# First set's weights converted one at a time, prepared weights fetched three products ahead, PSUM tiles evicted by one engine each

## The chip, the cores and the metric

The kernel runs on one core of a Trainium2 chip. The metric is device time in microseconds (us) of one execution. Engines are named as in the profile: PE (TensorE matmuls), PEld (TensorE weight loads), DVE (VectorE), ACT (ScalarE), POOL (GpSimd), and SP (SyncE), which here only issues DMAs; POOL issues accumulating DMAs as well. Each engine, and the DMA queue of SP and of POOL, works in its own program order.

## The reference

```python
def _attn_ref(q, k, v, omega):            # q, k, v: (4, 8, 576, 64); omega: (128, 64)
    ...                                   # phi(x) = exp(x omega^T - |x|^2/2 - max) / sqrt(m)
    kv = np.einsum('bhsm,bhsd->bhmd', k_p, v)
    z = np.sum(k_p, axis=2)
    num = np.einsum('bhsm,bhmd->bhsd', q_p, kv)
    den = np.einsum('bhsm,bhm->bhs', q_p, z)[..., None] + 1e-06
    return num / den

def _moe_ref(x, w_gate, w_val, w_out):    # x: (2304, 512); weights (512, 1536) and (1536, 512)
    g = x @ w_gate
    silu = g * (1.0 / (1.0 + np.exp(-g)))
    val = x @ w_val
    return (silu * val @ w_out).astype(np.float32)

def _moe2_ref(x, w_gate, w_val, w_out):   # the same with sigmoid alone as the gate
    ...

x = attention output as (2304, 512);  return _moe2_ref(_moe_ref(x))
```

The weights of both layers arrive as 64-bit floats and are converted to 32 bits on the chip.

## The kernel before

Attention runs first, in an order written out by hand. The 2304 tokens are then cut into three sets of 768, and each set passes through layer 0 and layer 1. A matmul of 32-bit values is done as three matmuls of a high and a low part: a copy on ACT makes the high part, a subtraction on DVE the low part (class `Split`, lines 238 and 242).

**The first set of layer 0** (the loop over `c` at line 783, 12 steps, one for each 128 columns of `d_ff`) multiplies directly. In a step PE computes two gate products (`first`, 12 matmuls of 384 columns each; ACT reads them for the SiLU into `s`, line 806), two value products (DVE multiplies `s` by them, line 812), and then `second` for the step before, which adds that step's part of the output into the six `acc` tiles. The four products of a step share two PSUM buffers (`ps_g`), so a product can start only when the product two before it has been read. ACT then makes `hh` of `s`, and DVE makes `hl`.

In the same loop the layer's weights are converted (class `Weight`): 26 units of 128x512, each loaded as 512 KB (`load`, line 136, into three `wraw` buffers), then `magnitude` on ACT (line 151, into one of four `wtmp` buffers), then `bits`, `sign`, `power` and `term` on DVE (lines 157, 164, 171, 177), and `total`, an accumulating DMA issued by POOL (line 183), which must land before the `wtmp` buffer is free again. Two or three units belong to a step, and they stand together at its end, each operation for all of them before the next operation. DVE also makes sums of weights (`sums`, line 214), and SP stores these and the weights to DRAM (`wf`, `ws`).

**The other five sets** (two of layer 0, three of layer 1) use Strassen products. For each of six `p` there are seven products `k` (line 950, 12 matmuls each, 42 in a set), then 12 steps of the output product (line 735 in layer 0, lines 260 to 262 in layer 1). PSUM holds two `X` tiles, one `Y` and one `Z`, of two banks each. Weights come back from DRAM: `fetch(o)` (line 714, SP, 256 KB, three `wp` buffers) and `prepare(o)`, which makes `vh` on ACT and `vl` on DVE. `prepare(o + 3)` is called at product `o` and fetches two further. Between the products the generator `make_second` converts layer 1's weights, one operation at a time. At a set's end `result` copies the six accumulators out, ACT and DVE in turn (lines 757 and 755); in layer 1 lines 1008 and 1010 do so.

Of the kernel before, what the change touches and what calls it, by code (L numbers as in the profile page):

```python
# [32 lines left out]
def tile_performer_attention__then__two_glu_layers(  # L33
# [230 lines left out]
    def first(ab, w, x, o):  # L264

        cols = slice(ab * TS, (ab + 1) * TS)
        for kk in range(KC):
            three(o, [u[:, kk, :] for u in w], [u[:, cols] for u in x[kk]], kk == 0, kk == KC - 1)
        return o
# [397 lines left out]
    }  # L667
    xc, xt, fetched, ready = {}, {}, {}, {}
    sequence = [
# [39 lines left out]
    def fetch(o):  # L709
        if o < len(sequence) and o not in fetched:  # L710
            l, p, k = sequence[o]
            t = fetched[o] = late.tile([P, 2 * H2], F32, tag="wp", bufs=3, name="wp")
            src = w_second[l][k] if p is None else w_first[l][p][:, k].rearrange("p n f -> p (n f)")
            nc.sync.dma_start(out=t, in_=src)

    def prepare(o):
        if o < len(sequence) and o not in ready:
            fetch(o)
            tags = slots[2 * (o % RING):2 * (o % RING) + 2]
            hi, lo = [wres.tile([P, 2 * H2], F32R, tag=x, name="v" + n) for x, n in zip(tags, "hl")]  # L720
            ready[o] = Split(fetched.pop(o), hi, lo).both()
            fetch(o + 1)
            fetch(o + 2)

# [22 lines left out]
    def result(acc, n, j):  # L747

        cols = set_of(n)
        src, dst = acc[j], xx[:, j % KC, cols.start:cols.start + MAIN]  # L750
        if j >= KC:
            src = src.rearrange("p (j t) -> p j t", j=2)
            dst = xx[:, 2 * (j - KC):2 * (j - KC) + 2, cols.start + MAIN:cols.stop]
        if j % 2:
            nc.vector.tensor_copy(dst, src)
        else:
            nc.scalar.activation(dst, src, AF.Copy)

    make = [[] for _ in range(FC)]
    for i, u in enumerate(units[0]):
        make[i * (FC - 3) // (len(units[0]) - 1)].append(u)
    done = {u.key for _, u in early}
# [11 lines left out]
    with tc.manual_schedule():  # L776
        for u in make[0]:
            u.load()
        prev = None
        acc = [ps_a.tile([P, MAIN], F32, tag=f"acc{j}", name="acc") for j in range(6)]  # L780
        late = pool("late", 1, side="right")
        for c in range(FC):
            for o, i in stores[c]:
                store(o, i)
            us = make[c]

            def part(us, *fs):
                for f in fs:
                    for u in us:
                        f(u)  # L790


# [9 lines left out]
            hl = hsb.tile([P, 2, TS], F32R, tag="hl", name="hl")  # L802
            place_of = lambda: ps_g.tile([P, TS], F32, tag="g", name="pg")
            for i in range(2):
                g = begun.pop(0) if begun else first(i, w[0], x, place_of())
                nc.scalar.activation(s[:, i], g, AF.Silu)  # L806
            values = [first(i, w[1], x, place_of()) for i in range(2)]
            for u in ahead:
                u.both()
            w2.both()  # L810
            for i in range(2):
                nc.vector.tensor_tensor(s[:, i], s[:, i], values[i], ALU.mult)
            nc.scalar.activation(hh, s, AF.Copy)
            t = wsum.tile([P, 4, H2], F32, tag="s", name="wsums")
            *_, then = sums(*pair, t)
            for o, i in then:
                store(o, i)
            nc.vector.tensor_tensor(hl, s, hh.bitcast(F32), ALU.subtract)
            x_parts(1, c - 2)
            part(us, Weight.magnitude, Weight.bits, Weight.sign, Weight.power, Weight.term)  # L820
            for u in us:
                u.total(True)
                store_later(c + 2, u)
                done.add(u.key)
            for u in make[c + 1] if c + 1 < FC else []:
                u.load()
            w2 = w2.parts
            w = w_next or [u.parts for u in ahead]
            if c >= FC - AHEAD:
                prepare(c + AHEAD - FC)  # L830
            if prev is not None:
# [6 lines left out]
        for j in LAST:  # L838
            result(acc, 0, j)
        for c in (FC - 2, FC - 1):  # L840
            x_parts(1, c)

# [3 lines left out]
        makers.close()  # L846
        wraw, wtmp, made = pool("wraw2", 2), pool("wtmp2", 3), pool("made", 1)
        ps_yz, ps_x = pool("ps_yz", 1, space=PSUM), pool("ps_x", 2, space=PSUM)
        tmp, hall = pool("tmp", 1), pool("hall", 1)
# [44 lines left out]
        def make_second():  # L894

            us, todo = units[1], []
            for u in us[:1]:
                u.load()
            yield
            for i, u in enumerate(us):  # L900
# [32 lines left out]
        for at, (layer, n) in enumerate(STRASSEN):  # L933
            h, hs = {}, {}
            ahead = STRASSEN[at + 1][1] if at + 1 < len(STRASSEN) else None
            for p in range(FC // 2):
# [5 lines left out]
                for k in range(7):  # L942
# [35 lines left out]
                    if p == FC // 2 - 1 and k in (3, 5):  # L978
                        c = (k - 3) // 2
                        hs[c] = h_split(c)  # L980
            acc = [bank(ps_yz, "Y"), bank(ps_yz, "Z"), bank(ps_x, "X")]
            acc = [t[:, i, :] for t in acc for i in range(2)]
# [19 lines left out]
            for b in range(6):  # L1002
# [3 lines left out]
                t = tmp.tile([P, DM], F32, tag=("u2", "p5", "s0", "s2")[b % 4], name="o")  # L1006
                if b % 2:
                    nc.scalar.activation(t, acc[b], AF.Copy)
                else:
                    nc.vector.tensor_copy(t, acc[b])  # L1010
# [46 lines left out]
```

## Time and profile before

| | us |
|---|---|
| median of three runs | 1054.29 (1053.64 to 1056.53) |
| the profiled execution, its own time | 1055.49 |
| its span from first to last instruction | 1053.7 |
| PE busy in the span | 1019.9 (97%) |
| DVE busy | 752.0 (71%) |
| ACT busy | 595.7 (57%) |

What the profiled execution takes beside its span is 1.79 us. PE's share of busy time is so high that only its gaps can be removed; where they lie is read from windows of the span, and what ends them from the waits and the timeline. The attention part ends at about 176 us of the span, the first set at about 344 us, and the last matmul starts at 1046.4 us.

### The profile page before, as it was taken

How to read it: one execution, taken by the hardware profiler on the slowest of the kernel's cores; microseconds unless marked ns; L12 is line 12 of the kernel's file. 1: busy time of each engine (PE TensorE's matmuls, PEld its weight loads, DVE VectorE, ACT ScalarE, POOL GpSimd, SP SyncE). 2: the span in 40 equal slices, each digit the busy share in tenths (PEclk: the TensorE clock that was granted, in tenths of full speed). 3: DMA queues.
4: the chain of work that ended last, by engine and by line, in shares of the span. 5: the costliest groups of instructions: out<-in, count | busy, mean ns of one | idle time of the engine just before them, and what ended most of it. 6: DMA issues, size and time to landing. Idle time of an engine off the chain costs nothing.

```text
span 1053.7 us, 17289 instructions
## 1 busy us (share of the span) xinstructions
PE 1019.9 (97%) x6079; PEld 956.8 (91%) x6079; DVE 752.0 (71%) x1526; ACT 595.7 (57%) x1259; POOL 86.4 (8%) x110
## 2 busy tenths in 40 slices
PE   8999999889999999999999999999999999999997
PEld 7999999889889989989899889898899998999985
DVE  6899996759785677887777886877655565556642
ACT  6999996324333655545555455655555554555532
POOL 2111112111110000000000000011000000000000
PEclk8999999999999999999999999999999999999999
DMA  7443422599794677756788666888244442444421
GB/s 204 137 127 111 107 81 81 157 238 258 215 263 142 172 221 225 213 163 179 199 239 251 172 178 197 259 245 214 81 150 131 130 114 67 141 130 125 117 79 61
DMA packets 138156, 173.15 MB, mean 164 GB/s; under 512 B 32852, under 2 KB 87124, under 8 KB 138068
## 3 DMA queue, kind: packets, MB, share of 16 engines
q1 hardware_dynamic: 129140, 155.78, 49.5%
q0 software_dynamic: 8928, 16.26, 8.6%
q8 instruction: 48, 0.79, 0.3%
q14 instruction: 40, 0.33, 0.1%
HBM read 122.72 MB, written 33.03 MB: 148 GB/s over the span
## 4 chain that ended last, share of the span: by engine, by line
PE 65%; DMA 11%; DVE 10%; issue 7%; ACT 4%; SPq 1%; POOL 0%; ACTq 0%; DVEq 0%; POOLq 0%
PE X L950 13%; PE Z L950 7%; DMA wp<-wf 6%; PE pj L420 4%; PE Y L950 4%; PE X L735 3%; PE Y L735 3%; PE kv L480 3%; PE Z L735 3%; ACT vh L238 3%; PE o L506 2%; DVE vl L242 2%; DMA raw<-in_moe_w_gate_dram 2%; PE acc L735 2%; DMA w<-mag 2%
## 5 line engine op out<-in xcount | busy, mean ns | idle before, releaser
L242 DVE TENSOR_TENSOR vl<-wp,vh 128x512 fp32r<-128x512 f32 x270 | 186.1, 689 | 147.6 <-ACT vh L238 147.3
L238 ACT ACTIVATE vh<-wp 128x512 fp32r<-128x512 f32 x270 | 167.5, 620 | 30.3 <-DMA wp<-wf 26.9
L950 PE MATMUL X<-xhi,vh 128*128 128x384 f32 x480 | 161.4, 336 | 5.6 <-DVE p L891 3.5
L950 PE MATMUL X<-xhi,vl 128*128 128x384 f32 x480 | 160.6, 335 | 0.1
L950 PE MATMUL X<-xlo,vh 128*128 128x384 f32 x480 | 160.4, 334 | 0.0
L882 ACT ACTIVATE hh<-h 128x768 fp32r<-128x768 f32 x60 | 50.6, 844 | 107.2 <-PE X L261 67.4
L883 DVE TENSOR_TENSOR hl<-h,hh 128x768 fp32r<-128x768 f32 x60 | 57.5, 958 | 64.9 <-ACT hh L882 64.7
L950 PEld LDWEIGHTS X<-xhi,vh 128*128 128x128 f32 x480 | 90.1, 188 | 8.9 <-issue 5.6
L950 PEld LDWEIGHTS X<-xhi,vl 128*128 128x128 f32 x480 | 90.1, 188 | 0.4 <-DVE vl L242 0.4
L950 PEld LDWEIGHTS X<-xlo,vh 128*128 128x128 f32 x480 | 90.1, 188 | 0.2
L950 PE MATMUL Z<-xhi,vh 128*128 128x384 f32 x240 | 81.4, 339 | 3.1 <-ACT vh L238 1.9
L950 PE MATMUL Z<-xhi,vl 128*128 128x384 f32 x240 | 81.5, 340 | 0.9
L950 PE MATMUL Z<-xlo,vh 128*128 128x384 f32 x240 | 80.3, 335 | 0.0
L151 ACT ACTIVATE mag<-raw 128x512 f32<-128x512 f32 x72 | 48.3, 673 | 38.5 <-DMA w<-mag 18.8
L260 PE MATMUL pg<-xhi,whi 128*128 128x384 f32 x160 | 56.1, 351 | 11.4 <-ACT s L806 11.4
L183 POOL DMA_DIRECT2D res<-mag x36 | 31.1, 864 | 385.2 <-DVE mag L177 370.1
L262 PE MATMUL pg<-xhi,wlo 128*128 128x384 f32 x160 | 55.5, 347 | 0.0
L261 PE MATMUL pg<-xlo,whi 128*128 128x384 f32 x160 | 55.5, 347 | 0.0
L950 PEld LDWEIGHTS Z<-xhi,vh 128*128 128x128 f32 x240 | 45.1, 188 | 6.0 <-ACT vh L238 4.2
L874 ACT ACTIVATE g<-p 128x384 f32<-128x384 f32 x30 | 15.8, 526 | 61.3 <-DVE p L891 61.3
L950 PEld LDWEIGHTS Z<-xhi,vl 128*128 128x128 f32 x240 | 45.0, 188 | 4.3 <-DVE vl L242 4.1
L177 DVE SCALAR_TENSOR_TENSOR mag<-raw,mag 128x512 f32<-128x512 uint32 x72 | 48.1, 687 | 0.8
(208 smaller groups left out, 2680.0 us busy)
## 6 DMA issues: line engine op xcount, KB each, us to landing
wp<-wf SPq DMA_DIRECT2D x210, 256.0 KB, 2.8
wp<-ws SPq DMA_DIRECT2D x60, 256.0 KB, 2.7
raw<-in_moe_w_gate_dram SPq DMA_DIRECT2D x24, 512.0 KB, 4.3
raw<-in_moe_w_val_dram SPq DMA_DIRECT2D x24, 512.0 KB, 4.4
raw<-in_moe_w_out_dram SPq DMA_DIRECT2D x24, 512.0 KB, 5.2
wf<-wsums SPq DMA_DIRECT2D x48, 256.0 KB, 4.8
res<-mag POOLq DMA_DIRECT2D x36, 256.0 KB, 5.2
w<-mag POOLq DMA_DIRECT2D x26, 256.0 KB, 8.6
```

The source lines that it names most:

```text
L151: nc.scalar.activation(self.mag, self.hi.bitcast(F32), AF.Abs, scale=REBIAS)
L177: nc.vector.scalar_tensor_tensor(self.mag, self.lo, 2.0**-52, self.mag, ALU.mult, ALU.mult)
L238: nc.scalar.activation(self.parts[0], self.src, AF.Copy)
L242: self.eng.tensor_tensor(lo, self.src, hi.bitcast(F32), ALU.subtract)
L260: nc.tensor.matmul(o, lhsT=l[0], rhs=r[0], start=start, stop=False)
L261: nc.tensor.matmul(o, lhsT=l[0], rhs=r[1], start=False, stop=False)
L262: nc.tensor.matmul(o, lhsT=l[1], rhs=r[0], start=False, stop=stop)
L420: nc.tensor.matmul(out_ap, lhsT=l[:, i, :], rhs=r, start=n == 0, stop=n == 2)
L735: nc.tensor.matmul(o, lhsT=l[a], rhs=r[b], start=start and i == 0 and not (tail and j % 2), stop=stop and i == 2, skip_group_check=tail,)
L882: nc.scalar.activation(hi, h[c], AF.Copy)
L883: nc.vector.tensor_tensor(lo, h[c], hi.bitcast(F32), ALU.subtract)
L950: nc.tensor.matmul(dst[:, i, :TS], lhsT=l[a], rhs=r[b], start=k in (0, 1) and kk == 0 and j == 0, stop=kk == 1 and j == 2, skip_group_chec ...
```

## The change

Four edits. The units of the first set are spread over 30 places, three in a step: before the second gate product's SiLU, before the value products' multiplication, and before `hl`. At each place one unit runs through all its DVE operations and then causes the load of the third unit after it. Where a step had its sums after the multiplication, it has them before. `prepare` in the last three steps, and the two last `x_parts`, move forward. The prepared weights get a fourth buffer and are fetched three ahead of the product being prepared. `result` and the last evictions give each two-bank tile to one engine, with `Z` first in the order. `make_second` starts four places later.

```diff
@@ fetch, prepare
-            t = fetched[o] = late.tile([P, 2 * H2], F32, tag="wp", bufs=3, name="wp")
+            at = more[0] if more and o % 4 == 3 else late
+            t = fetched[o] = at.tile([P, 2 * H2], F32, tag="wp", bufs=1 + 2 * (at is late), name="wp")
...
-            fetch(o + 1)
-            fetch(o + 2)
+            for i in range(2 + len(more)):
+                fetch(o + 1 + i)
@@ result
-        if j % 2:
+        if j // 2 != 0:
             nc.vector.tensor_copy(dst, src)
@@ first set
-    make = [[] for _ in range(FC)]
-    for i, u in enumerate(units[0]):
-        make[i * (FC - 3) // (len(units[0]) - 1)].append(u)
+    make = dict(((i * 29) // (len(units[0]) - 1), u) for i, u in enumerate(units[0]))
...
+            us = [make.get(3 * c + i) for i in range(3)]
+            def magnitude(i):
+                if us[i]:
+                    us[i].magnitude()
+            def rest(i):
+                u = us[i]
+                if u:
+                    for f in Weight.bits, Weight.sign, Weight.power, Weight.term:
                         f(u)
+                    u.total(True)
+                    load()
+                    store_later(c + 2, u)
+                    done.add(u.key)
...
+            magnitude(0)
             for i in range(2):
                 g = begun.pop(0) if begun else first(i, w[0], x, place_of())
                 nc.scalar.activation(s[:, i], g, AF.Silu)
-            values = [first(i, w[1], x, place_of()) for i in range(2)]
-            for u in ahead:
-                u.both()
-            w2.both()
-            for i in range(2):
-                nc.vector.tensor_tensor(s[:, i], s[:, i], values[i], ALU.mult)
-            nc.scalar.activation(hh, s, AF.Copy)
+                if i == 0:
+                    rest(0)
+                    w2.both()
+                    for u in ahead:
+                        u.both()
+                    if c >= FC - AHEAD:
+                        prepare(c + AHEAD - FC)
+            magnitude(1)
+            magnitude(2)
             t = wsum.tile([P, 4, H2], F32, tag="s", name="wsums")
             *_, then = sums(*pair, t)
             for o, i in then:
                 store(o, i)
+            rest(1)
+            for i in range(2):
+                o = first(i, w[1], x, place_of())
+                nc.vector.tensor_tensor(s[:, i], s[:, i], o, ALU.mult)
+            nc.scalar.activation(hh, s, AF.Copy)
+            rest(2)
             nc.vector.tensor_tensor(hl, s, hh.bitcast(F32), ALU.subtract)
-            x_parts(1, c - 2)
-            part(us, Weight.magnitude, Weight.bits, Weight.sign, Weight.power, Weight.term)
-            for u in us:
-                u.total(True)
...
@@ later sets
+        more.append(pool("more", 1))
...
-            yield
+            for _ in range(5):
+                yield
...
-            acc = [bank(ps_yz, "Y"), bank(ps_yz, "Z"), bank(ps_x, "X")]
+            acc = [bank(ps_yz, "Z"), bank(ps_yz, "Y"), bank(ps_x, "X")]
...
-                if b % 2:
+                if b // 2 == 0:
                     nc.scalar.activation(t, acc[b], AF.Copy)
```

PE's instructions keep their order in the first set. On ACT, from `hh` of step 0 to `hh` of step 1, this stood before (`mag` is a magnitude, `s` a SiLU that reads the gate product `pg`, `whi` a high part of weights):

```order
L813 ACTIVATE hh_3321<-s_3320 128x768
L151 ACTIVATE mag_3366<-raw64_3298 128x512
L151 ACTIVATE mag_3368<-raw64_3301 128x512
L151 ACTIVATE mag_3370<-raw64_3304 128x512
L806 ACTIVATE s_3402<-pg_3405 128x384
L806 ACTIVATE s_3402<-pg_3419 128x384
L238 ACTIVATE whi_3396<-w0_2_1800 128x512
L238 ACTIVATE whi_3398<-w1_2_2054 128x512
L238 ACTIVATE whi_3400<-w2_1_1489 128x512
L813 ACTIVATE hh_3403<-s_3402 128x768
```

Now the same stretch of ACT reads:

```order
L839 ACTIVATE hh_3321<-s_3320 128x768
L151 ACTIVATE mag_3405<-raw64_3332 128x512
L821 ACTIVATE s_3402<-pg_3407 128x384
L238 ACTIVATE whi_3400<-w2_1_1489 128x512
L238 ACTIVATE whi_3396<-w0_2_1800 128x512
L238 ACTIVATE whi_3398<-w1_2_2054 128x512
L821 ACTIVATE s_3402<-pg_3435 128x384
L151 ACTIVATE mag_3449<-raw64_3356 128x512
L151 ACTIVATE mag_3451<-raw64_3393 128x512
L839 ACTIVATE hh_3403<-s_3402 128x768
```

One magnitude instead of three stands ahead of a step's first SiLU, and the other two have moved behind its second. The magnitude of the very first unit has moved further, into the last pair of attention, and its four DVE operations with it.

On DVE, the units of one step stood together before:

```order
L157 TENSOR_SCALAR w1_3_3297<-mag_3366 128x512
L157 TENSOR_SCALAR w2_3_3300<-mag_3368 128x512
L157 TENSOR_SCALAR w0_4_3303<-mag_3370 128x512
L164 SCALAR_TENSOR_TENSOR w1_3_3297<-raw64_3298,w1_3_3297 128x512
L164 SCALAR_TENSOR_TENSOR w2_3_3300<-raw64_3301,w2_3_3300 128x512
L164 SCALAR_TENSOR_TENSOR w0_4_3303<-raw64_3304,w0_4_3303 128x512
L171 TENSOR_SCALAR mag_3366<-w1_3_3297 128x512
L171 TENSOR_SCALAR mag_3368<-w2_3_3300 128x512
L171 TENSOR_SCALAR mag_3370<-w0_4_3303 128x512
```

Now each unit's operations follow one another, here the second and the third unit of step 1, with the multiplication by the value products (`s`) between them:

```order
L157 TENSOR_SCALAR w2_4_3355<-mag_3449 128x512
L164 SCALAR_TENSOR_TENSOR w2_4_3355<-raw64_3356,w2_4_3355 128x512
L171 TENSOR_SCALAR mag_3449<-w2_4_3355 128x512
L177 SCALAR_TENSOR_TENSOR mag_3449<-raw64_3356,mag_3449 128x512
L838 TENSOR_TENSOR s_3402<-s_3402,pg_3470 128x384
L838 TENSOR_TENSOR s_3402<-s_3402,pg_3484 128x384
L157 TENSOR_SCALAR w0_5_3392<-mag_3451 128x512
L164 SCALAR_TENSOR_TENSOR w0_5_3392<-raw64_3393,w0_5_3392 128x512
L171 TENSOR_SCALAR mag_3451<-w0_5_3392 128x512
L177 SCALAR_TENSOR_TENSOR mag_3451<-raw64_3393,mag_3451 128x512
L841 TENSOR_TENSOR hl_3404<-s_3402,hh_3403 128x768
```

So each operation now reads what the one just before it wrote, and the multiplication stands behind a unit that it does not need.

## Rows read from the trace of the kernel before

**Rows 1.** Windows: us, each engine's busy us (instructions), PE clock, DMA share, GB/s.
```profile
158.00:176.00 18.00, 17.26 (x154) 16.14 (x153) 13.71 (x46) 14.27 (x47) 3.23 (x3) 1.00 0.29 89
200.00:320.00 120.00, 108.62 (x594) 102.79 (x593) 92.63 (x185) 44.89 (x83) 20.16 (x23) 0.97 0.87 239
250.00:260.00 10.00, 10.00 (x59) 9.51 (x58) 9.97 (x20) 4.69 (x9) 1.75 (x2) 1.00 1.08 316
345.00:745.00 400.00, 390.28 (x2175) 365.22 (x2174) 307.53 (x534) 222.17 (x385) 31.12 (x36) 1.00 0.73 206
745.00:1040.00 295.00, 295.00 (x1540) 274.25 (x1539) 168.89 (x254) 150.42 (x259) 0.00 (x0) 1.00 0.39 110
```

**Rows 2.** Waits in 176 to 345 us: who for whom, total us, times, longest.
```profile
ACT mag L151 <- DMA w<-mag: 18.8, 9, 2.4
...
PE pg L260 <- ACT s L806: 11.4, 6, 3.3
...
ACT mag L151 <- DMA raw<-in_moe_w_gate_dram: 10.2, 3, 3.5
```

**Rows 3.** Timeline of ACT: start, us, instruction, idle before and its releaser.
```profile
204.14 0.66 ACT L151 ACTIVATE mag<-raw 128x512 f32<-128x512 f32 x1 [3.28 <-DMA raw<-in_moe_w_gate_dram]
204.70 0.86 ACT L806 ACTIVATE s<-pg 128x384 f32<-128x384 f32 x2
```

**Rows 4.** Timeline of PE, the longest gap of the first set.
```profile
205.24 0.45 PE L260 MATMUL pg<-xhi,whi 128*128 128x384 f32 x1 [3.27 <-ACT s L806]
```

**Rows 5.** Windows of 2 us, columns as in rows 1.
```profile
206.00:208.00 2.00, 2.00 (x9) 2.00 (x8) 2.00 (x6) 1.12 (x3) 0.00 (x0) 0.50 0.00 2
...
224.00:226.00 2.00, 2.00 (x8) 2.00 (x8) 2.00 (x5) 0.00 (x0) 0.45 (x1) 0.50 0.00 0
```

**Rows 6.** Timeline of DVE, multiplications of steps 0, 10 and 11.
```profile
183.00 0.55 DVE L812 TENSOR_TENSOR s<-s,pg 128x384 f32<-128x384 f32 x1 [0.39 <-PE pg L262]
185.12 0.56 DVE L812 TENSOR_TENSOR s<-s,pg 128x384 f32<-128x384 f32 x1 [1.57 <-PE pg L262]
...
323.50 0.55 DVE L812 TENSOR_TENSOR s<-s,pg 128x384 f32<-128x384 f32 x1 [1.30 <-PE pg L262]
...
336.16 0.55 DVE L812 TENSOR_TENSOR s<-s,pg 128x384 f32<-128x384 f32 x1 [1.57 <-PE pg L262]
```

**Rows 7.** Timeline of DVE, three units together, and one unit alone.
```profile
261.74 0.43 DVE L157 TENSOR_SCALAR w<-mag 128x512 uint32<-128x512 uint32 x1 [0.89 <-ACT mag L151]
...
266.70 1.89 DVE L242 TENSOR_TENSOR wlo<-w,whi 128x512 fp32r<-128x512 f32 x3
...
314.94 0.42 DVE L157 TENSOR_SCALAR w<-mag 128x512 uint32<-128x512 uint32 x1
...
316.58 0.69 DVE L177 SCALAR_TENSOR_TENSOR mag<-raw,mag 128x512 f32<-128x512 uint32 x1
```

**Rows 8.** Timelines of SP and ACT, the last of three loads and its reader.
```profile
209.94 0.37 SPq L136 DMA_DIRECT2D raw<-in_moe_w_gate_dram  x1
...
220.48 0.66 ACT L151 ACTIVATE mag<-raw 128x512 f32<-128x512 f32 x1 [3.54 <-DMA raw<-in_moe_w_gate_dram]
```

**Rows 9.** Line 183: POOL's issue of an accumulating DMA (ns min/median/max), and its landing.
```profile
L183 POOL DMA_DIRECT2D w<-mag x26: 859/1146/1536, 192.7 to 317.6; - x26
...
DMA to landing us min/median/max: 3.5/8.6/11.7
```

**Rows 10.** Waits of PE in 345 to 1054 us, columns as in rows 2.
```profile
PE X L950 <- DVE p L891: 3.5, 6, 1.3
PE Z L950 <- ACT vh L238: 1.9, 5, 0.6
PE Z L950 <- DVE xx L755: 1.2, 2, 0.6
```

**Rows 11.** Waits of ACT in 345 to 760 us, and its longest wait for fetched weights.
```profile
ACT vh L238 <- DMA wp<-wf: 21.7, 20, 3.0
...
374.04 0.63 ACT L238 ACTIVATE vh<-wp 128x512 fp32r<-128x512 f32 x1 [3.02 <-DMA wp<-wf]
```

More of the change, by code (lines that the diff above doesn't have):

```diff
@@ L667, in tile_performer_attention__then__two_glu_layers @@
     }
-    xc, xt, fetched, ready = {}, {}, {}, {}
+    xc, xt, fetched, ready, more = {}, {}, {}, {}, []
     sequence = [
@@ L776, in tile_performer_attention__then__two_glu_layers, with load @@
     with tc.manual_schedule():
-        for u in make[0]:
-            u.load()
+        queue = list(units[0])
+        def load():
+            if queue:
+                queue.pop(0).load()
+        for _ in range(3):
+            load()
         prev = None
@@ L784, in tile_performer_attention__then__two_glu_layers @@
                 store(o, i)
-            us = make[c]
-            def part(us, *fs):
-                for f in fs:
-                    for u in us:
-                        f(u)
+            us = [make.get(3 * c + i) for i in range(3)]
[6 more added lines that the diff above has]
+                    for f in Weight.bits, Weight.sign, Weight.power, Weight.term:
+                        f(u)
+                    u.total(True)
+                    load()
+                    store_later(c + 2, u)
+                    done.add(u.key)
             w_next = w[2:]
@@ L817, in tile_performer_attention__then__two_glu_layers @@
                 store(o, i)
-            nc.vector.tensor_tensor(hl, s, hh.bitcast(F32), ALU.subtract)
-            x_parts(1, c - 2)
-            part(us, Weight.magnitude, Weight.bits, Weight.sign, Weight.power, Weight.term)
-            for u in us:
-                u.total(True)
[L823 to L826, printed above, removed]
+            rest(1)
[4 more added lines that the diff above has]
+            rest(2)
+            nc.vector.tensor_tensor(hl, s, hh.bitcast(F32), ALU.subtract)
+            for i in (c - 2, c - 1, c) if c == FC - 1 else (c - 2,):
+                x_parts(1, i)
             w2 = w2.parts
             w = w_next or [u.parts for u in ahead]
-            if c >= FC - AHEAD:
-                prepare(c + AHEAD - FC)
             if prev is not None:
@@ L839, in tile_performer_attention__then__two_glu_layers @@
             result(acc, 0, j)
-        for c in (FC - 2, FC - 1):
-            x_parts(1, c)
         banks.close()
```

## The prediction

> **What bounds the kernel now.** I read the windows first. In the last 300 us before the output (745 to 1040 us) PE is busy without a gap; in 345 to 745 us it is busy for 390.28 of 400 us, and in 200 to 320 us, inside the first set, only for 108.62 of 120 us [rows 1]. PE is the bound, and what can be won is its gaps: most in the first set, some in the sets after it, none behind.
>
> The waits say what ends the gaps in the first set: PE waits 11.4 us in six places for ACT's SiLU, and ACT waits 18.8 us for accumulating DMAs and 10.2 us for a gate load in front of its magnitudes [rows 2]. The timeline joins the two: ACT sits 3.28 us before a magnitude whose load has not landed, the SiLU stands behind that magnitude in ACT's order and starts at 204.70, and PE's next product, which needs the PSUM buffer that the SiLU reads, starts at 205.24 after 3.27 us of nothing [rows 3, 4]. The reader is to see a SiLU whose data was ready, held by the queue it stands in.
>
> PE then pays a second time. In the windows behind two of the gaps the granted clock is 0.50, that is 1.2 instead of 2.4 GHz [rows 5]. So I size the loss by the step's own length, not by the waits. Step 11 runs without a gap: its second multiplication follows that of step 10 by 336.16 - 323.50 = 12.66 us. Step 1 has no output product, so it needs four products of 185.12 - 183.00 = 2.12 us, 8.5 us. Eleven such steps are 8.5 + 10 x 12.66 = 135.1 us; they took 336.16 - 185.12 = 151.0 us [rows 6]. The first set loses **15.9 us**, and no edit to its waits can return more.
>
> In 345 to 745 us PE idles 400 - 390.28 = 9.7 us [rows 1]. A matmul is drawn until its modelled end, about 0.34 us, while a product of twelve takes 2.12 us, 0.18 us each; so a gap hides some 0.16 us more, for the 13 waits listed [rows 10] and as many small ones perhaps 3 us: some 12.5 us. The waits name DVE's `p` (an addition behind `vl` in DVE's order), ACT's `vh`, and the copy `xx` at a set's end [rows 10]; and ACT waits 21.7 us for fetched weights in the same stretch, at most 3.02 us at once [rows 11].
>
> **The change, part by part.** *Magnitudes.* One instead of three stands before a step's first SiLU. It needs a load that was caused a step earlier, after the unit whose buffer it takes: 12.66 us minus a unit's own 2.3 us, so some 10 us. The last of three loads issued together took from 209.94 to 220.48, 10.5 us [rows 8]; one at a time, with others in between, I expect less. The first SiLU may be 1.5 us late before PE notices, because the buffer is wanted one product (2.12 us) after its gate product ends. The other two magnitudes stand behind the second SiLU, where only `hh` and the next unit wait for them, and `hh` is wanted at the next step's output product, some 10 us on. An accumulating DMA takes at most 11.7 us and its issue 1.54 us [rows 9]; four buffers give a unit four thirds of a step, 16.9 us. I take the six gaps and the slow clock behind them as gone: -15.9 us. Below, nothing less than 0 if the loads still come too late.
>
> *Conversion on DVE.* A unit alone takes from 314.94 to 316.58 + 0.69 = 317.27, 2.33 us. Of three units together the last `bits` and the nine operations behind it take 266.70 - 261.74 = 4.96 us; with two more `bits` of at most 0.43 us that is at most 5.82, 1.94 us a unit [rows 7]. So one at a time costs at least 0.39 us more, and the 23 units between 200 and 320 us (POOL's 23 issues) 9 us. DVE was busy for 92.63 us there [rows 1]: 101.6 us in a window that shrinks to about 106, or 96%. What hides it is that DVE has no deadline tighter than the multiplication: the first must free its buffer before the next step's first product, 6.3 us after its value product ends. A unit and the sums now stand in front of it, so lateness of DVE above about 4 us at a step's start would reach PE. Free time of 4 us and 4 us of lateness are not much against waits for loads in between. I take 2 us of PE time, from 0 to the whole 9.
>
> The Trainium skill (VectorE: DVE Perf Modes, section "The DRAIN you can't avoid") says that chaining operations does not change what the engine spends between them. The trace shows otherwise, 2.33 against 1.94 us a unit [rows 7]. By the page these 2 us would be 0 and the second rival below half as likely.
>
> *First unit moved into attention.* Its magnitude (0.66 us on ACT [rows 3]) and its 2.33 us on DVE now stand in the last pair of attention. In 158 to 176 us ACT is busy 14.27 and DVE 13.71 of 18 us, PE 17.26 [rows 1]: both have some 4 us free, but PE does wait for them. Between 0 and 3.0 us; nearer to 0, I take +0.6.
>
> *Fetching three ahead.* No instruction is added. A fetch waits for the same buffer as before, but serves the product after: every fetch gains a product, 2.12 us. The longest of ACT's 20 waits shrinks from 3.02 to 0.9, the other 19 average (21.7 - 3.02) / 19 = 0.98 us and mostly vanish [rows 11]. What PE gets of this is bounded by its 12.5 - 1.2 = 11.3 us without the `xx` wait, and by 0 if ACT and DVE are late by their own work. Half of it, 6 us, since `p` and `vh` lead the list of PE's waits, and the conversions of layer 1 between the products remain. These also start four places later; nothing in them changes, and POOL's work ends before 745 us [rows 1], so I give it 0, with a few us if a store of layer 1's last weights comes late for its fetch.
>
> *Evictions.* `Z` is evicted first and by ACT alone, so the 1.2 us that PE waits for DVE's `xx` before `Z` [rows 10] go; DVE copies `X` and `Y` instead, and `Y` is wanted by a copy two products into the set. I take -1.0, between -1.2 and +1. At the very end six copies stay six copies: 0.
>
> *Moved `prepare` and `x_parts`* in the last steps: the fetches now stand ahead of a step's weight stores on SP, so ACT should find them landed; price 0, at worst one landing of some 3 us once.
>
> Sum: -15.9 + 2.0 + 0.6 - 6.0 - 1.0 = -20.3 us. Against the profiled execution's 1055.49 us that is 1035.2; the median of the runs lies 1.2 us below that execution, so I predict **1034.0 us**.
>
> **Rivals.** *A. The DMA engines cap the first set.* In 200 to 320 us their share is 0.87, 104 us of work; in 106 us it would be 0.98. For it: few windows are above that. Against it: 250 to 260 us shows 1.08 at 316 GB/s, and 104 / 1.08 = 97 us [rows 1]. If 0.93 is all that lasts, the window needs 112 us and 6 to 7 us are not returned: 1041.
>
> *B. DVE becomes the bound of the first set.* For it: 96%, in order, with waits between. If DVE idles a further 8 us behind loads and magnitudes, the set needs that longer: 1042.
>
> *C. The later sets keep their gaps*, because ACT and DVE are late by their load and not by fetches; then 6 us stay: 1040. Against it: the 21.7 us.
>
> *D. Slower: the unit in front of the multiplication.* The place is DVE's second unit of a step. If its load lands more than about 13 us after its issue (10 us of notice and 3 of slack), value products stay in PSUM, and PE's next gate product waits, in eight steps. Each us beyond costs 8 us; from 15.5 us on all that the change wins is lost: 1058 at 16 us. Against it: 10.5 us with three loads in flight.
>
> *E. It does not do what it says*: the three load buffers and the landing set the pace, each unit as late as before, and waits only change places: 1053.
>
> *F.* POOL's issue of an accumulating DMA takes 859 ns at best and up to 1536 ns in this set [rows 9]. If DVE, now nearly always busy, held each issue 5 us longer, a landing could come 18 us after the unit, 1 us more than four buffers give, in some steps: 2 to 4 us, 1037. This is the Trainium skill's rule (SBUF — State Buffer, section "Who interferes with whom") that two-port DVE operations lock GpSimd out of SBUF while it writes descriptors; the spread of the issues fits it, and the 5 us are not shown.
>
> **How the numbers follow.** Forecast (1029 to 1039.5): 0.60; A 0.07; B 0.12; C 0.08; D 0.05; E 0.05; F 0.03. The range 1028 to 1043 holds the forecast and A, B, C and F, 0.90, and leaves out D and E; the unknown costs (2 us of DVE from 0 to 9, 6 us of gaps from 0 to 11) stay within it unless all go one way. About 0.3%, 3.2 us, is what a measurement of this kernel tells from no change. Faster than 1051.1: all but D and E, 0.90; the same: E, 0.05; slower: D, 0.05.
>
> **What the profile after would show.** Right: in the first set no wait of PE for ACT's SiLU above 1 us, multiplications 12.7 us apart, no window at clock 0.50, DVE busy above 0.9; ACT's waits for `wp` below 5 us in total; no wait of `Z` for `xx`. Wrong: PE waiting for DVE's `s` in the first set (B, D), DMA share near 1 throughout with magnitudes waiting for loads (A, E), or PE's waits for `p` and `vh` unchanged while ACT's waits for `wp` are gone (C).

## The result and the profile after

The changed kernel takes 1025.3 us (median of 4 runs, 1023.75 to 1027.38) against 1055.32 us of the kernel before beside it: a ratio of 0.9725, 95% interval 0.9701 to 0.975, so some 29 us. The forecast was 1034.0 us, 20.3 us less, and its range ended at 1028; the time lies below it. The profiled execution spans 1024.8 instead of 1053.7 us, 28.9 less. (The kernel before ran again beside each batch of experiments, with medians from 1052.71 to 1056.09 us; each ratio below is to the runs beside it.)

The windows, columns as in [rows 1], at the same places of the span (the last one ends earlier, with the set):

```profile
158.00:176.00 18.00, 17.26 (x148) 16.00 (x148) 15.26 (x50) 14.51 (x45) 3.93 (x4) 1.00 0.31 98
200.00:320.00 120.00, 120.00 (x687) 115.58 (x686) 101.48 (x192) 47.73 (x89) 18.29 (x20) 1.00 0.87 235
345.00:745.00 400.00, 397.52 (x2209) 373.96 (x2208) 319.55 (x550) 225.17 (x394) 31.12 (x36) 1.00 0.74 208
745.00:1010.00 265.00, 264.45 (x1402) 248.38 (x1401) 149.49 (x224) 133.05 (x229) 0.00 (x0) 1.00 0.38 111
...
206.00:208.00 2.00, 2.00 (x13) 1.75 (x12) 1.90 (x5) 1.40 (x2) 0.00 (x0) 1.00 1.13 271
224.00:226.00 2.00, 2.00 (x13) 2.00 (x12) 1.31 (x3) 1.66 (x4) 0.75 (x1) 1.00 1.00 350
200.00:240.00 40.00, 40.00 (x230) 38.53 (x229) 35.07 (x66) 16.82 (x31) 7.19 (x8) 1.00 0.99 264
```

In the first set PE no longer has a gap (120.00 of 120 us), and the clock of 0.50 is gone. The loss of 9.7 us in 345 to 745 us is down to 2.5, and behind that stands a small new one, 0.55 us, where [rows 1] show none. The DMA share is 0.99 from 200 to 240 us, and PE does not wait there.

The timeline of DVE, multiplications of steps 0 and 11, as in [rows 6]:

```profile
183.88 0.55 DVE L838 TENSOR_TENSOR s<-s,pg 128x384 f32<-128x384 f32 x1 [0.34 <-PE pg L262]
...
319.34 0.56 DVE L838 TENSOR_TENSOR s<-s,pg 128x384 f32<-128x384 f32 x1 [1.63 <-PE pg L262]
```

The first multiplication of all stands at 182.99 (183.00 before), the last at 319.34 (336.16 before): 16.8 us less between them. As a mark for PE this is not good enough, because in the changed kernel step 0's multiplications stand behind units on DVE. PE's first matmul of the set's 48 products and its last one, before and then with the change:

```profile
175.45 0.44 PE L260 MATMUL pg<-xhi,w 128*128 128x384 f32 x1
...
335.79 0.34 PE L262 MATMUL pg<-xhi,wlo 128*128 128x384 f32 x1
```
```profile
174.21 0.44 PE L260 MATMUL pg<-xhi,w 128*128 128x384 f32 x1
...
318.89 0.34 PE L262 MATMUL pg<-xhi,wlo 128*128 128x384 f32 x1
```

So the products of the first set take 144.7 instead of 160.3 us, 15.7 us less, and PE comes to them 1.2 us earlier. The 1.2 us show nothing of the change: kernels with the same code up to there differ by 1.4 us in this start (174.13 to 175.54 us among those with the first set's edit, 174.20 to 175.45 among those without).

The waits of PE from 327 us on, where [rows 10] named three others, and those of ACT from 327 to 760 us for DMAs, as [rows 11]:

```profile
PE Z L260 <- DVE u L905: 1.5, 3, 0.9
PE X L965 <- DVE p L905: 1.2, 2, 0.9
```
```profile
ACT mag L151 <- DMA raw<-in_moe_w_out_dram: 2.8, 2, 1.5
ACT vh L238 <- DMA wp<-wf: 2.7, 2, 1.7
```

ACT's waits for fetched weights fell from 21.7 to 2.7 us, and PE's waits for `vh` and `xx` are gone. New is the wait of the output product's `Z`: with `Z` first it starts in the tile that DVE's addition `u` has only just read. One such place on PE and on DVE, the end of the last product of layer 1's first set (here a conversion's `term`, line 177, stands ahead of `u` as well, so that PE loses 1.20 us; in the two sets behind it 0.45):

```profile
693.84 0.34 PE L965 MATMUL X<-xhi,vl 128*128 128x384 f32 x1
695.13 0.47 PE L260 MATMUL Z<-vh,hh 128*128 128x512 f32 x1 [0.95 <-DVE u L905]
```
```profile
693.43 0.68 DVE L177 SCALAR_TENSOR_TENSOR mag<-raw,mag 128x512 f32<-128x512 uint32 x1
694.03 0.95 DVE L905 TENSOR_TENSOR u<-Z,u 128x768 f32<-128x768 f32 x1
```

To compare the later sets without the ends that the records model, I take the starts of matmuls. In the last two sets of layer 1 the last matmul of the 42 products starts 87.21 us after the first one, in every kernel here; what a set takes beyond that is its loss. (The wait for `Z` in front of the output product comes after that matmul and is not in it.) For the three sets behind the first the losses were 4.48, 6.53 and 7.10 us, and are 1.05, 1.82 and 1.26. With the set boundaries (start of the second set to start of the fifth, 344.32 to 773.89 before, 327.43 to 744.20 now) the three sets give 12.8 us; the last two take 1.0 us longer. So 1.2 + 15.7 + 12.8 - 1.0 + 0.2 (the tail) is the 28.9 us of the spans, where the forecast had 13.3 for the first set and attention and 7.0 for the rest.

### The profile page after: what moved, and what is told of

It reads as the page before. It is cut to its first block, busy times and chain, and to the rows that moved or that the text cites. A ratio compares the mean times of both kernels' runs of the same rounds, so it can differ in the third digit from the quotient of the medians.

```text
span 1024.8 us, 17314 instructions
## 1 busy us (share of the span) xinstructions
PE 1009.6 (99%) x6079; PEld 954.0 (93%) x6079; DVE 765.2 (75%) x1532; ACT 590.5 (58%) x1253; POOL 86.9 (8%) x110
## 4 chain that ended last, share of the span: by engine, by line
PE 88%; DVE 4%; ACT 3%; issue 2%; DMA 2%; SPq 0%; POOL 0%; ACTq 0%; DVEq 0%; POOLq 0%
PE X L965 20%; PE Z L965 10%; PE Y L965 6%; PE acc L736 5%; PE pj L420 4%; PE X L736 3%; PE Z L736 3%; PE pg L260 3%; PE Y L736 3%; PE pg L262 3%; PE pg L261 3%; PE kv L480 3%; PE o L506 2%; PE Z L260 2%; PE Z L262 2%
```

## The experiments

In the table "first" is the time from the first to the last multiplication of the first set, the mark by which the expectations were written; "products" is the time from PE's first to its last matmul of that set's products, and the gains and losses of the first set below are read from it. "Losses" are those of the next three sets as defined above. All three are of the one profiled execution of each kernel; "ratio" is to the kernel before.

| kernel | us | ratio, 95% | first | products | losses |
|---|---|---|---|---|---|
| before | 1055.32 | | 153.17 | 160.34 | 4.48, 6.53, 7.10 |
| the change | 1025.3 | 0.9725 (0.9701 to 0.975) | 136.35 | 144.69 | 1.05, 1.82, 1.26 |
| only_first | 1037.17 | 0.9853 (0.9814 to 0.9892) | 136.35 | 144.68 | 3.22, 5.37, 6.42 |
| only_fetch | 1047.05 | 0.9944 (0.9924 to 0.9965) | 153.69 | 160.86 | 5.07, 2.76, 2.40 |
| only_evict | 1055.2 | 1.0021 (1.0001 to 1.0042) | 153.51 | 160.69 | 2.73, 4.45, 8.58 |
| only_delay | 1049.58 | 0.997 (0.9951 to 0.9989) | 153.80 | 160.97 | 3.29, 3.78, 3.47 |
| no_first | 1040.42 | 0.9887 (0.9862 to 0.9913) | 153.13 | 160.31 | 0.53, 0.16, 1.25 |
| no_fetch | 1035.1 | 0.981 (0.978 to 0.984) | 136.35 | 144.68 | 3.16, 3.07, 5.00 |
| no_delay | 1030.33 | 0.9767 (0.9742 to 0.9791) | 136.36 | 144.69 | 5.76, 0.66, 1.63 |
| y_first | 1023.55 | 0.9701 (0.9678 to 0.9724) | 136.35 | 144.69 | 0.62, 0.82, 1.28 |
| mags_ahead | 1032.7 | 0.9787 (0.9757 to 0.9817) | 143.60 | 152.38 | 0.24, 0.40, 1.25 |
| power2 | 1030.19 | 0.9777 (0.9761 to 0.9793) | 139.58 | 149.19 | 0.14, 0.14, 1.25 |
| power3 | 1041.3 | 0.9883 (0.9868 to 0.9899) | 149.93 | 160.20 | 1.74, 0.43, 1.26 |
| together | 1041.76 | 0.9884 (0.9865 to 0.9904) | 154.69 | 161.80 | 0.76, 0.89, 1.27 |
| grouped | 1047.76 | 0.9947 (0.9929 to 0.9965) | 157.26 | 164.36 | 0.24, 1.25, 1.24 |
| together_hl | 1051.71 | 0.9979 (0.9961 to 0.9996) | 162.12 | 169.22 | 0.69, 0.27, 1.27 |
| grouped_hl | 1061.46 | 1.0083 (1.0063 to 1.0102) | 173.20 | 180.31 | 0.46, 0.38, 1.25 |

One thing must be seen before the rest: kernels with the same code behind the first set differ by up to 2.6 us in their losses (the change 4.1 in sum, power2 1.5), since small shifts in time decide which load is late. Differences below that are read from single places only.

**One edit alone.** *only_first*, *only_fetch*, *only_evict* and *only_delay* are the kernel before with the hunks of one of the four edits, as the diff above groups them.

> The kernel before with the edit of the first set alone (units one at a time at three places, prepare and x_parts moved forward). My theory, that the later sets' 12 us come from the fetches: -17 us, about 1038 us, the 12 multiplications of the first set as close together as with the whole change (319.3 - 183.0 us), and the sets behind it with their gaps, ACT waiting some 20 us for wp in them. Rival 1, that the moved prepare and x_parts or the earlier stores also clear later gaps: -20 to -24 us, and ACT's waits for wp fall below 10 us. Rival 2, that the evictions or the later conversions matter for the first set as well: less than -15 us.

It came as my theory had it: the whole 15.7 us in the first set's products, 3 us behind it, and ACT still waits 19.4 us for `wp` there.

> The kernel before with the fetches three ahead (fourth buffer) alone. My theory: ACT's waits for wp behind the first set fall from 21.7 us to below 3, PE's gaps there from some 14 us of lost starts to about 4, and the time by 9 to 11 us, to about 1045. The prediction's price: 6 us, 1049. Rival, that ACT and DVE are late by their own work (the prediction's rival C): the waits for wp go and PE's gaps stay, less than 2 us.

The time fell by 5.7 us, near the prediction's 6, and not by my 9 to 11. ACT's waits for `wp` behind the first set fell to 2.3 us, and PE's waits for `vh` are gone, so the rival falls. But one place lost what others won; the waits of PE from 345 us on, and of ACT from 345 to 760 us:

```profile
PE X L952 <- ACT u L889: 3.2, 1, 3.2
PE Z L952 <- DVE xx L756: 1.2, 2, 0.6
PE X L952 <- DVE p L893: 0.5, 2, 0.3
```
```profile
ACT mag L151 <- DMA raw<-in_moe_w_gate_dram: 8.5, 4, 5.4
...
ACT vh L238 <- DMA wp<-wf: 2.3, 3, 1.0
```

In products 3 and 4 of the second set 3.37 and 1.50 us are lost: ACT's copy `u` stands behind the magnitude of layer 1's first unit, which waits 5.4 us for its load. Without these 4.87 us the losses would be 5.36 in sum, 12.8 less than before. (The profiled execution of the kernel before lies 2.8 us above the median beside these runs, so by medians its losses are somewhat smaller than in the trace.)

> The kernel before with the evictions alone (one engine to a tile, Z first). My theory and the prediction: PE no longer waits for xx at the two set boundaries, -1 us, not to be told from 0 by the time; read from the trace. Rival, that the evictions also clear the products behind a boundary: -3 us or more.

At the two set boundaries the loss at product 0 fell from 0.79 and 0.80 us to 0.03 each; in layer 1 the last product now loses 1.20, 0.44 and 0.44 us, where it lost 0.08 us in the first of these sets and nothing in the others. The sum is a loss of 0.5 us; the time shows 0.2% more, with an interval from 0.01% to 0.42%.

> The kernel before with layer 1's conversions started four places later, alone. My theory and the prediction: 0 us, every gap of PE behind the first set about as before. Rival, that the place of a conversion among the products sets which of DVE's and ACT's operations come late: -3 us or more, with gaps of PE gone at products where a conversion stood before.

The rival's 3 us came, so the price of 0 was wrong: 3.1 us faster, and 7.6 us less of losses in the profiled execution, while most of ACT's waits for `wp` from 300 to 760 us stay (21.3 us; 26.9 before). What it clears alone these numbers do not say. The next runs show what it does beside the fetches.

**The change without one edit.** Each of these is the changed kernel with the hunks of one edit undone; the evictions were not taken out in this way, only the order of the output tiles (below).

> The changed kernel with layer 1's conversions started as early as before. Alone, the later start won 3.1 us and the fetches 5.7 us, of which the fetch-only profile lost 4.9 us again in one place: products 3 and 4 of the second set waited for a copy on ACT that stood behind layer 1's first magnitude, whose load stood behind three fetches on SP. Theory 1: the fetches clear nearly all gaps by themselves, and the later start only clears that one stall; then it stands here again, some 4 to 5 us slower than with the whole change, 1029 to 1031, and PE loses nothing new elsewhere. Theory 2: the later start moves DVE's work away from products that need it; then gaps of 0.3 to 1.2 us come back in all three sets, 5 us or more in sum, and none is above 2 us. Theory 3: the prepare moved forward in the first set has taken the fetches ahead of that load already: the same time as with the whole change, 1025.

Theory 1 holds. The timelines of SP, ACT and PE at the start of the second set (327.36 us):

```profile
317.66 14.46 SPq L715 DMA_DIRECT2D wp<-wf  x2
332.17 0.98 SPq L136 DMA_DIRECT2D raw<-in_moe_w_gate_dram  x2
```
```profile
336.26 0.66 ACT L151 ACTIVATE mag<-raw 128x512 f32<-128x512 f32 x1 [5.22 <-DMA raw<-in_moe_w_gate_dram]
336.82 0.79 ACT L901 ACTIVATE p<-Z 128x768 f32<-128x768 f32 x1
337.51 0.62 ACT L238 ACTIVATE vh<-wp 128x512 fp32r<-128x512 f32 x1
338.03 0.80 ACT L901 ACTIVATE u<-X 128x768 f32<-128x768 f32 x1
```
```profile
338.89 0.45 PE L964 MATMUL X<-xhi,vh 128*128 128x384 f32 x1 [3.02 <-ACT u L901]
```

The fetches on SP hold the raw load until 332.17 us; the magnitude waits for it, the copies `p` and `u` behind the magnitude, and PE for `u`. Here it costs 3.19 + 0.86 + 0.82 us in products 3 to 5. The last two are the clock, as in [rows 5]: behind the idle stretch 0.55 and 0.60 were granted, close to the lower of its two levels, 1.2 GHz. Windows of 2 us of this kernel:

```profile
336.00:338.00 2.00, 0.00 (x0) 0.00 (x0) 0.00 (x0) 1.74 (x3) 0.00 (x0) 1.00 0.79 287
...
340.00:342.00 2.00, 2.00 (x9) 2.00 (x8) 1.62 (x4) 0.26 (x1) 0.00 (x0) 0.55 0.63 175
342.00:344.00 2.00, 2.00 (x9) 2.00 (x8) 1.42 (x2) 0.94 (x2) 0.00 (x0) 0.60 0.68 210
```

In the changed kernel the same load leaves as late (332.24 us), but the magnitude stands four places of the generator later (339.99 us on ACT) and does not wait.

> The changed kernel with three buffers and fetches two ahead. Theory 1 (the fetches clear nearly all gaps): ACT waits some 20 us for wp again, PE loses some 11 us in the products of the three sets instead of 5.8, +5 us, about 1030. Theory 2 (with the later start the fetches are worth little): within 2 us of the whole change.

ACT waits 16.6 us for `wp`, and the losses are 11.2 instead of 4.1 us; by the time some 9 us slower than the whole change (0.981 against 0.9725). Theory 1, at nearly twice its price of 5 us.

> The changed kernel without the edit of the first set: fetches, evictions and later conversions alone. Expected from the parts: first set 153.5 us as before; the three sets behind it as with the whole change, 417 us, if their gain does not hang on the first set's edit, and then 1025 + 17 = 1042; or, if the moved prepare and x_parts are needed for it, 3 us or more in the first products of the second set, 1045 or more.

The three later sets keep their whole gain (losses of 1.9 us in sum): it does not hang on the first set's edit.

**Order of the output tiles.** In layer 1 the order of before returns:

```diff
-            acc = [bank(ps_yz, "Z"), bank(ps_yz, "Y"), bank(ps_x, "X")]
+            acc = [bank(ps_yz, t) for t in ("YZ" if layer else "ZY")] + [bank(ps_x, "X")]
```

> The changed kernel with layer 1's output products in the order Y, Z, X as before, and layer 0's with Z first. My theory: the output product of layer 1 starts in Z, which DVE's addition u has only just read, and Y had been free for long; so the losses of 1.20, 0.45 and 0.45 us at the last product of each layer 1 set go to below 0.1 each, 2 us faster, 1023; in the time this is 0.2% and hardly to be told. Rival: Y first makes the next set's Z wait for DVE's copy: what is won there is lost at the start of the next set.

The losses at the last product of layer 1's sets go from 1.20, 0.45 and 0.44 to 0.08, 0.00 and 0.00 us, and the start of the next sets loses nothing for it. Its median is the lowest of all kernels here; by the intervals of the ratios alone it can't be told from the whole change, the places in the trace can.

**What the first set's gain is made of.** *mags_ahead* puts the three magnitudes of a step where they stood before, with the spread units kept:

```diff
-            magnitude(0)
+            for i in range(3):
+                magnitude(i)
             for i in range(2):
                 g = begun.pop(0) if begun else first(i, w[0], x, place_of())
...
-            magnitude(1)
-            magnitude(2)
```

> The changed kernel with all three magnitudes of a step ahead of its first SiLU, as they stood before; units still spread over three places. The prediction's mechanism (the SiLU is held by magnitudes behind it whose loads are late): the loads of the second and third unit are caused in the step before some 9 and 5 us ahead of these magnitudes and take 4 to 9 us, so the SiLU is late by up to 3 us beyond its slack of about 1.5 us: PE waits for s in several steps, 5 to 20 us slower, 1030 to 1045. Rival: with the loads caused one by one they have landed by then, and the order on ACT no longer matters: 1025, no wait of PE for s.

The products of the first set lose 7.7 of the 15.7 us that they had gained, and PE waits for the SiLU again as in [rows 2], in a smaller size:

```profile
PE pg L260 <- ACT s L822: 5.3, 3, 3.2
```

So the place on ACT is worth 7.7 us once the units are spread, and the spread the other 8.0. ACT's 18.8 us in front of magnitudes for accumulating DMAs [rows 2] are gone in both of these kernels; what is left in *mags_ahead* are 25.2 us for loads. The next four runs ask what it is worth alone, and what is left when the units stand together. *together* moves `rest(0)` and `rest(1)` to `rest(2)`, behind `hh`; *grouped* moves all magnitudes behind the second SiLU and gives `rest` all units of the step at once, so that it converts operation by operation and causes the loads at the end, as before; its core:

```diff
-            magnitude(0)
...
+            for i in range(3):
+                magnitude(i)
...
-            rest(2)
+            rest([u for u in us if u])
             nc.vector.tensor_tensor(hl, s, hh.bitcast(F32), ALU.subtract)
```

> The changed kernel with the DVE work of all three units of a step behind hh, still one unit after the other, and each load still caused behind its unit; magnitudes as changed. Theory (what counts is the order on ACT and when the loads are caused, not the three places on DVE): multiplications come earlier, hl some 5 us later, and hl is wanted some 10 us after hh: the first set as long as with the whole change, 136.4 us, 1025. Rival: the loads of the next step are caused later, and the magnitude ahead of its first SiLU comes late: PE waits for s, 3 to 10 us slower.

> The changed kernel with the conversions of the first set as before (three units together, operation by operation, behind hh, loads of the next three caused at the end), but all three magnitudes behind the second SiLU. It takes the order on ACT alone from the first set's edit. Theory (a SiLU held by magnitudes behind it is the whole loss): 136 to 138 us from the first to the last multiplication, 1025 to 1027. Rival (spreading the loads is needed as well, since hh now stands behind the magnitudes): hh and so hl come late, PE waits in the output product: 5 us or more slower.

Both theories fell: the whole gain of the first set is lost, and more. PE waits for ACT's SiLU in both (11.5 and 13.8 us), as the rival to the first had it. But both runs had a second fault. `s` has one buffer, `hl` reads it, and `hl` now stood behind the units; in *grouped* ACT's SiLU waited 31.0 us for `hl`. So both were run again with `hl` ahead of the units:

> As the run with the three units of a step together behind hh, but with hl ahead of them. There the first set took 154.7 us; ACT's magnitudes waited 38 us for loads, 7 SiLUs of PE were late. Theory 1 (hl behind the units was the cause): 136 to 140 us, 1026 to 1030. Theory 2 (the loads are caused too late for the magnitude ahead of the next SiLU): 148 us or more, magnitudes waiting 30 us or more for loads, 1037 or more.

> As the run with the conversions grouped, but with hl ahead of the three units on DVE, as it stood before the change; so it takes from the first set's edit the place of the magnitudes on ACT alone. In the grouped run the SiLU waited 31.0 us for hl, which reads the one buffer s that the SiLU writes and stood behind three units. Theory 1 (the place on ACT is enough once hl is not held): 136 to 139 us from the first to the last multiplication, 1026 to 1030. Theory 2 (loads caused together come too late wherever the magnitudes stand; only spreading them helps): the wait moves to hh and whi, which stand behind the magnitudes, and from there to hl and s: 145 us or more, 1034 or more.

Worse again, as theory 2 had it for both, so `hl` was not the cause. The waits of PE, ACT and DVE in *grouped_hl*, 176 to 340 us:

```profile
DVE hl L837 <- ACT hh L836: 39.7, 10, 8.5
...
PE pg L260 <- ACT s L820: 24.7, 6, 12.8
ACT mag L151 <- DMA raw<-in_moe_w_gate_dram: 22.0, 6, 6.0
ACT mag L151 <- DMA raw<-in_moe_w_val_dram: 21.2, 4, 7.9
ACT mag L151 <- DMA raw<-in_moe_w_out_dram: 19.4, 4, 5.9
ACT mag L151 <- DMA w<-mag: 12.2, 4, 3.8
```

This is a ring: magnitudes wait for loads and for accumulating DMAs, `hh` stands behind the magnitudes, `hl` waits for `hh`, the units stand behind `hl`, and the next loads and accumulating DMAs behind the units. With the SiLU moved ahead of its own step's magnitudes, `hh` stood behind them, and the next step's SiLU behind `hh`; PE waited 24.7 us for it.

What these four runs do not part is loads caused together from loads caused too late. Moving the magnitudes or the units also left less time between a load's issue and its magnitude than with the change. In *grouped_hl*, on SP and on ACT:

```profile
211.04 0.37 SPq L136 DMA_DIRECT2D raw<-in_moe_w_val_dram  x1
```
```profile
215.02 0.68 ACT L151 ACTIVATE mag<-raw 128x512 f32<-128x512 f32 x1 [5.96 <-DMA raw<-in_moe_w_val_dram]
```

ACT was free for this magnitude at 209.06 us, 2.0 us before its load was issued. From the issue of a load of the first set to the moment at which ACT was free for its magnitude 4.7 to 9.0 us passed in the kernel before (median 5.5 of the last 23 loads), and 3.9 to 14.7 us (median 8.45) with the change. So the change shortens the landings and also leaves more time for them, and no run tells how much each is worth.

**How much DVE time was free.** *power2* and *power3* compute `power` two and three times in each unit of the first set; the output is the same.

```diff
-                    for f in Weight.bits, Weight.sign, Weight.power, Weight.term:
+                    for f in Weight.bits, Weight.sign, *[Weight.power] * 2, Weight.term:
```

> The changed kernel with one more DVE operation in each unit of the first set: power is computed twice (same output). Such an operation takes 0.46 us from start to start, so some 1.4 us more per step of three units, 9 us in 80 us. DVE is busy for 72.5 of the 80 us from 200 to 280 us with the change. Theory 1 (only DVE's free time counts, and lateness costs nothing until it is used up): 0 to 2 us slower, 1025 to 1027, first set's multiplications 136.4 to 138 us. Theory 2 (the prediction's: lateness of DVE reaches PE before DVE is full, which is why 2 us were priced for 9 us of work): with 9 us more at least 4 us slower, 1029 or more.

> The changed kernel with two more DVE operations in each unit of the first set (power three times), some 2.8 us more per step. Theory 1: the free time of 1.2 us per step is used up, and what is beyond it, 1.6 us in each of some eight steps, reaches PE: 10 to 14 us slower, 1035 to 1039, PE waiting for DVE's s. Theory 2: more than twice what one more operation costs. Rival: still nothing, because steps with two units (10 of 12 have less than three or no layer sums) give it back: below 3 us.

25 units of 0.46 us are 11.5 us more work each time. The first 11.5 us cost the first set's products 4.5 us, the next 11.0. So some 7 us of DVE time were free, and beyond that nearly every us reaches PE. The waits of PE in the first set for *power3*:

```profile
PE pg L260 <- DVE s L838: 8.0, 6, 2.6
PE pg L260 <- ACT s L821: 4.0, 7, 0.7
```

The first operation more is just as theory 2 had it: 4.5 us in the products and 4.9 us by the median, where it said at least 4 and theory 1 at most 2. For *power3* the two theories do not exclude each other: PE does wait for DVE's `s`, but 15.5 us in the products and 16.0 by the median are above theory 1's 10 to 14, and more than twice the first step, as theory 2 said.

## Why the prediction was wrong, step by step

*The first set's gaps, -15.9: right in size and in mechanism, but not the whole mechanism.* All six gaps and the slow clock went, for 15.7 us by PE's products; "no edit to its waits can return more" held. The account of why was incomplete. I named the SiLU held by a magnitude, and the place of the magnitudes is worth 7.7 us (mags_ahead); but that holds with the units spread, and in the two runs without it the set got longer (grouped, grouped_hl). The spread is worth the other 8.0 us; with it ACT no longer waits for accumulating DMAs in front of its magnitudes. Landings became shorter too; they had been up to 10.5 us for a raw load and 11.7 us for an accumulating DMA [rows 8, 9]. In the changed kernel, first for line 136 from 176 to 345 us, then for line 183 from 170 to 345 us:

```profile
DMA to landing us min/median/max: 3.8/4.6/6.9
```
```profile
L183 POOL DMA_DIRECT2D w<-mag x26: 859/862/1057, 173.3 to 297.1; - x26
...
DMA to landing us min/median/max: 3.3/6.1/7.7
```

*One unit at a time, +2.0: at most 0.4.* PE's steps start 12.65 or 12.66 us apart, as a step without a gap did before (12.66); only step 1 took 13.04. The price of a unit was right; one unit alone in the changed kernel:

```profile
266.62 0.42 DVE L157 TENSOR_SCALAR w<-mag 128x512 uint32<-128x512 uint32 x1
267.07 0.69 DVE L164 SCALAR_TENSOR_TENSOR w<-raw,w 128x512 uint32<-128x512 uint32 x1
267.80 0.43 DVE L171 TENSOR_SCALAR mag<-w 128x512 uint32<-128x512 uint32 x1
268.26 0.69 DVE L177 SCALAR_TENSOR_TENSOR mag<-raw,mag 128x512 f32<-128x512 uint32 x1
268.87 1.01 DVE L838 TENSOR_TENSOR s<-s,pg 128x384 f32<-128x384 f32 x2
```

That is 2.25 us from start to the next start, against at most 1.94 with three together. The Trainium skill (VectorE: DVE Perf Modes, section "The DRAIN you can't avoid") says that chaining operations without semaphores does not save the time between them, from copies with and without semaphores. Here operations that need each other's output are 0.3 us a unit slower than ones that do not. So to read the rule as "these 2 us would be 0" is wrong for DVE's work, though PE's time came out near it. What failed is the step from work to time: "Free time of 4 us and 4 us of lateness are not much". They were enough: DVE was busy for 72.5 of 80 us from 200 to 280 us, 0.91 and not the forecast 0.96, DVE's 26.1 us of waits for magnitudes before are no wait now, and power2 and power3 show some 7 us still free. Rival B was only as far away as that.

*The first unit in attention, +0.6: not to be seen.* PE's first product starts at 174.21 against 175.45 us, within the 1.4 us by which kernels with the same code differ.

*Fetching three ahead, -6: too small, and with the next step the one that failed most.* I took half of PE's loss "since `p` and `vh` lead the list of PE's waits". The list names what came last; `vh` and `p` were late because ACT had waited for `wp`. With the fetches alone PE's losses fall by 12.8 us but for one stall of 4.87, and the time, with that stall, by 5.7; without the fetches the whole change loses 7.1 us more in the three sets, some 9 us by the time. So alone the edit was worth the 6 us only because a stall took the rest back. Beside the later conversions it is worth 7 to 9 us, the two together some 12 (the 12.8 us of the three sets without the evictions' share), and rival C is refuted.

*The later conversions, 0: with the fetches a gain of some 5 us.* "Nothing in them changes" overlooked SP's queue: a raw load behind fetches that wait for buffers, and in ACT's order copies of PSUM behind its magnitude. The fetch edit makes this stall and the later start takes it away (no_delay). Alone, without the third fetch, the later start also wins 3.1 us; which transfers it parts there is not settled, and beside the fetches there is nothing left of it.

*Evictions, -1.0: +0.5.* The boundaries gave 1.5 us, a little more than the 1.2 that were read for them, and layer 1 took back 1.12 + 0.45 + 0.44. The step looked at who empties `Z` and not at who last reads it before the output product starts there; y_first shows both halves.

*The moved `prepare`, 0:* from the last multiplication to the second set it takes 8.08 instead of 8.15 us.

Rival A is refuted: a share of 0.99 over 40 us held no magnitude up. Rivals D and E did not occur. Rival F neither: ACT waited for no accumulating DMA, and none landed later than 7.7 us after its issue, with DVE busier than before. So the rule cited for it from the Trainium skill (SBUF — State Buffer, section "Who interferes with whom") leaves no mark here. The spread of POOL's issues that I took as fitting it (up to 1536 ns) belongs to issues in a row, whose records overlap: before, the three from 241.81 us on took 2.63 us together, 0.88 each. Of the miss of 8.6 us by the spans, 3.6 are in the first set and attention: 1.2 of an earlier start that runs of the same code also show, and prices for work that stayed hidden. The other 5.0 are behind it: the fetches and the later conversions gave some 6 us more than forecast, the evictions 1.5 less.

## What to carry to other kernels

Where loads feed an in-order engine, look for the ring (load, its reader, what stands behind the reader, and what frees the next buffer): here moving one reader shifted the wait to the next in line, and spreading the loads, each with more time before its reader, took the ring apart. The last releaser in a list of waits is often late itself; before a prefetch is priced at half, ask what that releaser waited for. And an edit that starts a transfer earlier may sit in a queue ahead of another load: it pays in full only with the edit that moves that load's reader.

## What the runs showed of the hardware unexpectedly

Landings of the same transfers became shorter when they were issued one by one, at the same mean DMA share of 0.87 over 200 to 320 us: the longest raw load took 6.9 instead of 10.5 us, the longest accumulating DMA 7.7 instead of 11.7. It goes with the way of issuing and not with the rest of the change: in *grouped*, three together, the longest took 10.5 and 10.7 us; in *together*, whose first set is no faster than before but which issues them one after the other, 7.5 and 8.5.
